# A fused S4D and MLP-mixer kernel: layer 1's operands moved to one place modulo 256 bytes, and a new order of layer 2's products

## The chip, the core and the metric

The kernel runs on one core of one Trainium2 chip. The metric is the device time of one execution in microseconds (us). All names of engines are those of the profile: PE is the matrix engine, PEld its weight loads, DVE the vector engine, ACT the scalar engine with its function tables, POOL the GpSimd engine, SP the sync engine, which here only issues DMAs.

## The reference

For 2048 tokens of 576 features, the reference normalizes the input twice and sends it through two branches. One is an S4D convolution (a long convolution with a kernel made from complex exponentials, done with FFTs), the other a two-layer MLP with a hidden width of 4608. The branches are multiplied and added to the input.

```python
x = A_u                                     # 1 x 2048 x 576, float32
xn = _layernorm(x)
s = S4D(xn, log_A_real, A_imag, C_real, C_imag, log_dt, D_skip)   # FFT convolution over the tokens
y = _layernorm(xn)
h = gelu(einsum("bsd,df->bsf", y, w1) + b1)       # 576 -> 4608, tanh form
g = silu(einsum("bsf,fd->bsd", h, w2) + b2)       # 4608 -> 576
return x + s * g
```

## The kernel before

**The MLP's arithmetic.** A float32 value is cut into a high part, which the matrix engine reads as `float32r`, and a low part, the rest. Every product of two float32 matrices is then three products on PE: high by high, high by low, low by high. `XH` and `XL` are the transposed normalized tokens (four blocks of 128 features), `XR` holds the last 64 features, its high part on partitions 0 to 63 and its low part on 64 to 127. `w1h`, `w1l`, `w1r` and `w1s` are the parts of `w1`, `w2h` and `w2l` those of `w2`, `hh` and `hl` those of the hidden values.

**Slots.** The hidden width is worked off in 12 groups of 384 (`G` = 3 blocks of 128), twice: once for the first 1024 tokens, once for the other 1024. Each group handles two token blocks of 512 (`TB`), so there are 48 slots. A slot has two layers:
- Layer 1 (`layer1`, L512; in slot 0 `first_layer1`, L527 to L533): three hidden blocks, each of 14 matmuls of 128x512. The moving operand is a slice of `XH`, `XL` or `XR`, the stationary one a 128-column slice of `w1h`, `w1l`, `w1r` or `w1s`. These 14 add up in one bank of PSUM. Then `hidden` makes a gelu on ACT (L545), a copy into `hh` on ACT (L548), and a subtraction into `hl` on DVE (L551).
- Layer 2 (`layer2`, L569): for each of four sets `j` of 128 tokens, 18 matmuls of 128x288: three hidden blocks `i` by two halves `dh` of the 576 output columns by the three products of parts. The moving operand is a half row of `w2h` or `w2l`, the stationary one a 128-column slice of `hh` or `hl`. DVE adds the sum to `acc` (L577).

`l2_terms` gives the order of layer 2. For the first two token sets it has four pieces: set 0 with the hidden blocks 0 and 1 (12 matmuls), the beginning of set 1 with them, set 0 with block 2, the rest of set 1. Sets 2 and 3 follow, a half at a time. The reason is that block 2 leaves layer 1 last, so its gelu, copy and subtraction run while the first pieces are multiplied.

**What is fitted in between.** The S4D branch (tables of sines and exponentials on ACT and DVE, small matmuls at L889, L962, L1000, L1053 and L1080, FFT products on DVE) and the splitting of the weights (L489 on DVE, L492 on ACT) are cut into steps, and the class `Order` places them while the kernel is traced. It keeps planned times of each engine. A hidden value's steps are urgent; another step of ACT or DVE is placed only if it would end, by the plan, before the next urgent step of that engine is due (`advance`; the due times come from `hidden_by` and `add_by`, which add up the planned lengths `LEN` of the PE pieces). The resulting order on each engine is fixed; the chip then runs each engine in that order, with waits. The test for ACT charges 1.28 us per table load:

```python
                    if st["tbl"]:
                        d += 1.28 * (1 + (st["tbl"] != self.tbl))
                    if b > horizon or b + d > soon.get(e, 1e9) + st["late"]:
                        continue
```

So a step that names a table pays for one load back, and for one load more if another table is in; a step that names none (copies, absolute values, weight splits) pays nothing.

**Where the operands lie.** The tiles lie in SBUF in the order in which the trace first asks for them. As the kernel is built, `XH`, `XL`, `XR` and `w1s` start 192 bytes past a multiple of 256 in each partition; `w1h`, `w1l` and `w1r` start 64 bytes past one. All slices of them that the matmuls read are whole multiples of 256 bytes further on. `w2h`, `w2l`, `hh` and `hl` start 64 bytes past a multiple of 256; the first half of an output row of `w2h` or `w2l` (`dh` = 0) stays there, and the second half (`dh` = 1) begins 1152 bytes on, at 192.

Of the kernel before, what the change touches and what calls it, by code (L numbers as in the profile page):

```python
# [9 lines left out]
F32 = mybir.dt.float32  # L10
# [7 lines left out]
L, D, N, F = 2048, 576, 128, 4608  # L18
P = 128
# [16 lines left out]
G = 3  # L36
# [18 lines left out]
class Order:  # L55
# [83 lines left out]
    def advance(self, horizon):  # L139
        while True:  # L140
            best = None
            soon = dict(self.next)
            for u in self.urgent:
                st = u[1][0]
                k = (max(u[0], self.t[st["eng"]]), 0)
                if u[0] <= horizon and (best is None or k < best[0]):
                    best = (k, u, None)
                for st in u[1]:
                    soon[st["eng"]] = min(soon.get(st["eng"], 1e9), st["by"])
            for x in self.lines:  # L150
                if x["steps"] and x["steps"][0]["by"] < 1e9:
                    st = x["steps"][0]
                    soon[st["eng"]] = min(soon.get(st["eng"], 1e9), max(st["by"], self.t[st["eng"]] + st["dur"]))
            for n, x in enumerate(self.lines):
                h = self.head(x)
                if h is None or h[0]["eng"] == "PE":
                    continue
                st, r = h
                if st["eng"] is None:
                    k = (max(r, 0), 1 + n)  # L160
                    if r > horizon:
                        continue
                else:
                    e = st["eng"]
                    b = max(self.t[e], r)
                    d = st["dur"]
                    if st["tbl"]:
                        d += 1.28 * (1 + (st["tbl"] != self.tbl))
                    if b > horizon or b + d > soon.get(e, 1e9) + st["late"]:
                        continue  # L170
                    k = (b, 1 + n)
                if best is None or k < best[0]:
                    best = (k, None, x)
            if best is None:
                break
            if best[1] is not None:
                self.go(best[1])
            else:
                self.run(best[2])
            self.pin()  # L180
# [31 lines left out]
def mixer_kernel(ctx, tc, u, log_a_real, a_imag, c_real, c_imag, log_dt, d_skip, w1, b1, w2, b2,  # L212
                 f1, f2, g2, g1, tvals, ident, out, parts=("mlp", "s4d")):
    nc = tc.nc
    sb = ctx.enter_context(tc.tile_pool(name="sb", bufs=1))
# [5 lines left out]
    def bank2(name):  # L221
        return ps.tile([P, 2, TB], F32, name=name, bufs=2 if name == "cv" else 1)
# [6 lines left out]
    def tok(t, b, p0=0, n=P):  # L229
        return dram(t, (b + 16 * p0) * D, [[16 * D, n], [1, D]])  # L230
# [24 lines left out]
    tv, small = tvs[:, :NV], tvs[:, NV:]  # L255
    b1t = sb.tile([P, F // P], F32, name="b1t")
    halfpi, epst = small[:, 0:2], small[:, 2:4]
    w1s = sb.tile([P, G * P], F32R, name="w1s")

    def load_tv():  # L260
# [53 lines left out]
    nc.vector.memset(epst[:, 0:1], EPS)  # L314
    nc.vector.memset(epst[:, 1:2], EPS * EPS)
    nc.vector.memset(w1s[64:].bitcast(F32), 0.0)


    YT, XT = {}, {}
# [28 lines left out]
    def norms(b0, n):  # L348

        def stats(t, part=None):
            if part == 1:
                pass
            elif t == 0 and b0 in (1, 3):
                MV[b0] = SECOND.pop()
            elif t == 0:
                a, r = (UV[:, D + 8 * b0 + 8 * k:D + 8 * b0 + 8 * k + 8] for k in range(2))
                a, r = a.rearrange("p (t k) -> p t k", k=2), r.rearrange("p (k t) -> p k t", k=2)
                MV[b0] = a[:, :n], r[:, :, :n]  # L360
                if n == 1:
                    SECOND.append((a[:, 1:2], r[:, :, 1:2]))
                    PAIR[b0 + 1] = r[:, :, :2]
            if part != 1:
                MV["st"] = sb.tile([P, 2, 6], F32, name="st")
            st = MV["st"]
            for i in range(2) if part is None else (part,):
                nc.vector.bn_stats(st[:, i], XT[b0 + t][:, i * 288:(i + 1) * 288])
            if part != 0:
                nc.vector.bn_aggr(MV[b0][0][:, t], st)  # L370

        def roots():
            mv, rs = MV[b0]
            nc.scalar.activation(rs[:, 0], mv[:, :, 1], AF.Sqrt, bias=epst[:, 0:1], scale=1.0)
            nc.scalar.activation(rs[:, 1], mv[:, :, 1], AF.Sqrt, bias=epst[:, 1:2], scale=1.0 + EPS)

        def recip():
            nc.vector.reciprocal(MV[b0][1], MV[b0][1])

        def second(t):  # L380
            mv, rs = MV[b0]
            y = sb.tile([P, D], F32, name="row", bufs=NROW)
            nc.vector.tensor_scalar(y, XT[b0 + t], mv[:, t, 0:1], rs[:, 1, t:t + 1], op0=OP.subtract, op1=OP.mult)
            if b0 >= 8:
                nc.sync.dma_start(y_s[b0 + t - 8], y)
            else:
                YT[b0 + t] = y

        def first(t):
            mv, rs = MV[b0]  # L390
            x = XT.pop(b0 + t)
            nc.gpsimd.tensor_scalar(x, x, mv[:, t, 0:1], rs[:, 0, t:t + 1], op0=OP.subtract, op1=OP.mult)
            nc.gpsimd.dma_start(tok(xn_s, b0 + t), x)
        return stats, roots, recip, second, first
# [1 line left out]
    XH = sb.tile([P, KB, 2, TB], F32R, name="XH")  # L396
    XL = sb.tile([P, KB, 2, TB], F32R, name="XL")
    XR = sb.tile([P, 2, TB], F32R, name="XR")
    dsk = sb.tile([P, D // 4], F32, name="dsk")
    nc.vector.memset(dsk, 0.0)  # L400

    def y_load(b):
        y = sb.tile([P, D], F32, name="row", bufs=NROW)
# [59 lines left out]
    def w1_tiles():  # L463
        W[1] = (sb.tile([P, KB, G * P], F32R, name="w1h"), sb.tile([P, KB, G * P], F32R, name="w1l"),
                sb.tile([P, G * P], F32R, name="w1r"), w1s)
# [32 lines left out]
    def mx(i):  # L498
        return "mxa" if (turn[0] + i) % 2 == 0 else "mxb"
# [54 lines left out]
    def layer2(g, tb, j, terms, last, alone=False):  # L554

        h, lo = W[2]
        hh, hl = HID[tb]
        c = slice(j * P, (j + 1) * P)  # L560
        if alone and terms[0][1]:
            Q2[j] = bank2("cv")
        elif j not in Q2:
            Q2[j] = bank2(mx(j + 1))
        q = Q2[j]
        for i, dh in terms:
            d = slice(dh * 288, dh * 288 + 288)
            for k, (a, b) in enumerate(((hh, h), (hh, lo), (hl, h))):
                nc.tensor.matmul(q[:, dh, :288], a[:, i, c], b[:, i, d], start=i == 0 and k == 0,  # L569
                                 stop=i == G - 1 and k == 2)  # L570
        if last:
            Q2.pop(j)

        def add(dh, n):
            o = acc[:, tb * 4 + j].rearrange("p (h d) -> p h d", h=2)[:, dh:dh + n]
            b = bias2.rearrange("p (h d) -> p h d", h=2)[:, dh:dh + n]
            nc.vector.tensor_add(o, q[:, dh:dh + n, :288], b if g == 0 else o)  # L577
        return add
# [554 lines left out]
    def warm_up(n):  # L1133
        for _ in range(n):
            nc.tensor.matmul(qb[:, 0], zero[:, :P], zero, start=True, stop=True)
    warm_up(22)
    na = [norms(b, 1) for b in range(4)]
    na[0][0](0)
    w1_tiles()

    nc.gpsimd.tensor_copy(small[:, 4:5], MV[0][0][:, 0, 0:1])
    nc.gpsimd.dma_start(idp, dram(ident, 0, [[P, 64], [64 * P, 2], [1, P]]))
# [43 lines left out]


    L1 = 14 * 0.2315
    LEN = [L1] * G + [3 * n * 0.132 + 0.02 for n in (4, 2, 2, 4, 3, 3, 3, 3)]

    T0 = 12.5
    for e, t in dict(PE=0.0, ACT=4.6, DVE=3.7, POOL=3.8, SP=0.0).items():
# [46 lines left out]
    def weigh_in(which):  # L1239

        m = KB + 1 if which == 1 else G
        end = od.t["PE"] + sum(LEN[G:] if which == 1 else LEN[:G])
        for i in range(m):
# [126 lines left out]
    def l2_terms(k):  # L1370

        if k < 4:
            a = [(i, dh) for dh in range(2) for i in range(G - 1)]
            b = [(G - 1, dh) for dh in range(2)]
            return ((0, a, False, range(G - 1)), (1, a[:2], False, range(G - 1)),
                    (0, b, True, (G - 1,)), (1, a[2:] + b, True, range(G)))[k]
        j, dh = k // 2, k % 2
        return j, [(i, dh) for i in range(G)], dh == 1, range(G)

    def when(pos, q):  # L1380

        return od.t["PE"] + sum(LEN[k % NPOS] for k in range(pos + 1, q))

# [24 lines left out]
    for slot in range(NSLOT):  # L1408
        turn[0] = slot + 1
        g, tb = slot // 2 % NG, slot % 2  # L1410
        n = slot // 2
        final = slot >= NSLOT - 2
        for pos in range(NPOS):
# [19 lines left out]
            else:  # L1433
                j, terms, last, hid = l2_terms(pos - G)
# [8 lines left out]
                halves = slot == NSLOT - 1 and j == 3  # L1443
                od.unit(lambda: cell.append(layer2(g, tb, j, terms, last, halves)), LEN[pos], need)
                look_ahead(pos)
                if last or halves:
                    add = cell[0]
                    dh, k = (terms[0][1], 1) if halves else (0, 2)
                    done = ("acc", slot, j, dh)
                    chain = [step("DVE", dve(288 * k), lambda: add(dh, k), mark=done, by=add_by(pos, j))]  # L1450
                    if final:
                        b = 8 + 4 * tb + j
                        x = el if slot < NSLOT - 1 else od.line()
                        st = finish(b, dh * 288, (dh + k) * 288, slot == NSLOT - 1, slot == NSLOT - 1 and j > 1)
# [69 lines left out]
```

## Time and profile before

| | |
|---|---|
| median of 3 runs (lowest, highest) | 1108.05 us (1106.91, 1109.93) |
| the profiled execution's own time | 1107.08 us |
| its span, first to last instruction | 1105.3 us |
| granted clock of PE | 0.999 |
| busy: PE, PEld, DVE, ACT, POOL | 99%, 85%, 85%, 59%, 18% |

The profile shows one execution. [...] The distance between the starts of two matmuls that follow each other is what one of them costs. The view of waits tells who sat idle and what ended the idle time; the chain tells what the end was waiting for, step by step.

### The profile page before, as it was taken

What the parts mean: (1) busy time and instruction counts of PE and PEld (TensorE: products, weight loads), DVE (VectorE), ACT (ScalarE), POOL (GpSimd) and SP (SyncE); (2) the same over time, 40 slices, a digit from 0 to 9 for tenths busy, and PEclk for the clock granted to TensorE, in tenths of its full rate; (3) what the DMA queues carried; (4) which work ended last, traced back from release to release, by engine and by line L of the source; (5) the groups of instructions that cost most, each with busy time, mean ns of one, the idle gap of its engine ahead of it and who ended that gap; (6) DMA issues with size and microseconds to landing.
All of it is one profiled execution on the core that took longest, in us unless ns stands there. A gap on an engine that the chain in (4) does not pass through costs nothing.

```text
span 1105.3 us, 27245 instructions
## 1 busy us (share of the span) xinstructions
PE 1088.8 (99%) x11547; PEld 941.5 (85%) x11547; DVE 940.9 (85%) x1510; ACT 657.1 (59%) x977; POOL 197.9 (18%) x282
## 2 busy tenths in 40 slices
PE   9999999999999999999999999999999999999997
PEld 7889989888888888888888888888888888888896
DVE  7799698978999999989699998999999976666466
ACT  6666688666656556657866755665764733233333
POOL 5584532011000200010100001000100021110231
PEclk9999999999999999999999999999999999999999
DMA  8645557333233231633322322233412455342254
GB/s 244 224 147 182 192 205 209 103 107 114 65 87 83 72 93 40 140 94 99 106 85 89 69 77 78 67 98 49 125 22 95 109 139 179 87 127 83 60 186 114
DMA packets 111513, 125.54 MB, mean 114 GB/s; under 512 B 59940, under 2 KB 82032, under 8 KB 110368
## 3 DMA queue, kind: packets, MB, share of 16 engines
q1 hardware_dynamic: 95728, 76.44, 24.7%
q0 software_dynamic: 15104, 46.49, 13.6%
q8 instruction: 90, 1.47, 0.5%
q10 hardware_dynamic: 560, 0.89, 0.3%
q14 instruction: 31, 0.25, 0.1%
HBM read 95.52 MB, written 34.01 MB: 117 GB/s over the span
## 4 chain that ended last, share of the span: by engine, by line
PE 84%; DVE 11%; ACT 2%; issue 2%; DMA 1%; SPq 0%; DVEq 0%; ACTq 0%
PE mxb L569 19%; PE mxa L569 19%; PE mxa L512 19%; PE mxb L512 16%; PE cv L889 3%; PE cv L1000 3%; PE cv L1053 2%; PE cv L962 2%; DVE hl L551 1%; DVE w2l L489 1%; DVE acc L577 1%; PE cv L1080 1%; DVE mg L832 1%; DVE A L949 1%; DVE w L807 1%
## 5 line engine op out<-in xcount | busy, mean ns | idle before, releaser
L569 PE MATMUL mxa<-w2h,hl 128*128 128x288 f32 x573 | 170.0, 297 | 4.0 <-DVE hl L551 4.0
L569 PE MATMUL mxb<-w2h,hh 128*128 128x288 f32 x576 | 171.6, 298 | 0.0
L569 PE MATMUL mxa<-w2h,hh 128*128 128x288 f32 x573 | 171.0, 298 | 0.3 <-DVE acc L577 0.3
L569 PE MATMUL mxb<-w2h,hl 128*128 128x288 f32 x576 | 170.2, 296 | 0.0
L569 PE MATMUL mxb<-w2l,hh 128*128 128x288 f32 x576 | 169.5, 294 | 0.0
L569 PE MATMUL mxa<-w2l,hh 128*128 128x288 f32 x573 | 168.6, 294 | 0.0
L551 DVE TENSOR_TENSOR hl<-h,hh 128x512 fp32r<-128x512 f32 x144 | 98.7, 687 | 73.4 <-ACT hh L548 72.9
L789 POOL DMA_DIRECT2D par<-par_s x36 | 27.4, 761 | 533.0 <-DVE mg L832 520.1
L545 ACT ACTIVATE h<-mxa,b1t 128x512 f32<-128x512 f32 x73 | 50.0, 687 | 117.0 <-PE mxa L512 115.1
L569 PEld LDWEIGHTS mxb<-w2h,hh 128*128 128x128 f32 x576 | 108.1, 188 | 8.6 <-issue 2.9
L569 PEld LDWEIGHTS mxa<-w2h,hh 128*128 128x128 f32 x573 | 107.5, 188 | 7.9 <-issue 2.3
L569 PEld LDWEIGHTS mxa<-w2h,hl 128*128 128x128 f32 x573 | 107.6, 188 | 5.6 <-DVE hl L551 5.6
L569 PEld LDWEIGHTS mxb<-w2l,hh 128*128 128x128 f32 x576 | 108.2, 188 | 0.8
L569 PEld LDWEIGHTS mxa<-w2l,hh 128*128 128x128 f32 x573 | 107.7, 188 | 0.8
L569 PEld LDWEIGHTS mxb<-w2h,hl 128*128 128x128 f32 x576 | 108.1, 188 | 0.0
L545 ACT ACTIVATE h<-mxb,b1t 128x512 f32<-128x512 f32 x71 | 48.9, 688 | 91.3 <-PE mxb L512 90.3
L548 ACT ACTIVATE hh<-h 128x512 fp32r<-128x512 f32 x144 | 90.8, 631 | 4.2
L492 ACT ACTIVATE w2h<-raw 128x576 fp32r<-128x576 f32 x72 | 44.5, 675 | 63.2 <-PE mxa L569 63.1
L577 DVE TENSOR_TENSOR acc<-mxb,acc 128x576 f32<-128x576 f32 x88 | 65.8, 748 | 17.5 <-PE mxb L569 17.3
L512 PE MATMUL mxa<-XH,w1h 128*128 128x512 f32 x284 | 79.3, 400 | 0.5 <-DVE acc L577 0.5
L512 PE MATMUL mxb<-XH,w1h 128*128 128x512 f32 x280 | 78.7, 402 | 0.5 <-ACT h L545 0.5
L577 DVE TENSOR_TENSOR acc<-mxa,acc 128x576 f32<-128x576 f32 x88 | 65.4, 743 | 15.9 <-PE mxa L569 15.5
(235 smaller groups left out, 2483.6 us busy)
## 6 DMA issues: line engine op xcount, KB each, us to landing
raw<-in_B_w_dram SPq DMA_DIRECT2D x72, 288.0 KB, 3.2
raw<-in_B_w_dram SPq DMA_DIRECT2D x96, 192.0 KB, 2.9
par_s<-A POOLq DMA_DIRECT2D x8, 1080.0 KB, 4.8
par<-par_s POOLq DMA_DIRECT2D x36, 240.0 KB, 3.3
f2t<-f2q SPq DMA_DIRECT2D x24, 256.0 KB, 3.4
raw<-in_B_w_dram SPq DMA_DIRECT2D x48, 96.0 KB, 3.3
u_s<-in_A_u_dram POOLq DMA_DIRECT2D x16, 288.0 KB, 4.4
xc<-xn_s SPq DMA_DIRECT2D x48, 96.0 KB, 3.9
```

Of the source, the lines that this page charges most:

```text
L492: nc.scalar.activation(h, r, AF.Copy)
L512: nc.tensor.matmul(q, a, b, start=j == 0, stop=j == len(ops) - 1)
L545: nc.scalar.activation(t, q, AF.Gelu_apprx_tanh, bias=b1t[:, g * G + i:g * G + i + 1], scale=1.0)
L548: LAST[0] = nc.scalar.activation(hh[:, i], t, AF.Copy)
L551: nc.vector.tensor_sub(hl[:, i], t, hh[:, i].bitcast(F32))
L569: nc.tensor.matmul(q[:, dh, :288], a[:, i, c], b[:, i, d], start=i == 0 and k == 0, stop=i == G - 1 and k == 2)
L577: nc.vector.tensor_add(o, q[:, dh:dh + n, :288], b if g == 0 else o)
L789: nc.gpsimd.dma_start(PAR[b].rearrange("p (g i) k -> p g (i k)", g=4), dram(par_s, (b // 6 * CH + b % 6 * 4) * NPAR, [[D * NPAR, P], [24 * ...
L889: nc.tensor.matmul(q[32 * g:32 * g + 32, i // 2, i % 2 * 64:i % 2 * 64 + 64], U[:, ri, 4 * g + i, :], v[:, ri, 4 * g + i, :], start=ri == ...
L962: nc.tensor.matmul(Q1ST[i, x][g // 2][64 * f:64 * f + 64, g % 2].rearrange(order), f1t[r].rearrange("p s k -> p (s k)"), rhs(r, f), start= ...
L1000: nc.tensor.matmul(Q[i][32 * q:32 * q + 32, f, 2 * ri:2 * ri + 2], m[r, 4 * i + q, 32 * ri:32 * ri + 32], A2[r, 4 * p + 2 * i + q // 2, :, ...
L1053: nc.tensor.matmul(QI[q // 2][64 * f:64 * f + 64, q % 2, i], MAT["g2t", p + i // 2][r, i % 2, ri], YS[p + i // 2][0][r, i % 2, ri, f], sta ...
```

## The change

Four edits, and the lengths that go with them:
- `dsk` (576 bytes in a partition) is allocated and cleared before `w1s` instead of after `XR`. Everything in between moves up by 576 bytes, which is 64 past a multiple of 256: `w1s`, `XH`, `XL`, `XR`, and with them `A2`, `acc` and `U`, which are used by the S4D branch and the sums.
- The tiles of `w1` are made before the first statistics (`st`, 48 bytes), so that `w1h`, `w1l` and `w1r` move down by 64 bytes. As the changed kernel is built, all seven operands of layer 1 start at a multiple of 256 bytes. `w2h`, `w2l`, `hh` and `hl` stay where they were.
- In layer 2, set 1 takes three (block, half) pairs, nine matmuls, before set 0's last block instead of two pairs, six matmuls. And in each piece the products with the low part of block 2 (`hl`, `i` = 2) come last. `LEN` follows: 4, 3, 2, 3 in place of 4, 2, 2, 4.
- `Order.advance` charges an ACT step for a load if its table is not the one that is in, and for another if the table after it is not that of gelu or silu; a step without a table is charged too, where the table that is in is another than these.

```diff
-                    if st["tbl"]:
-                        d += 1.28 * (1 + (st["tbl"] != self.tbl))
+                    if e == "ACT":
+                        after = st["tbl"] or self.tbl
+                        d += 1.28 * ((after != self.tbl) + (after not in ("gelu", "silu")))
...
+    dsk = sb.tile([P, D // 4], F32, name="dsk")
     w1s = sb.tile([P, G * P], F32R, name="w1s")
...
+    nc.vector.memset(dsk, 0.0)
...
     XR = sb.tile([P, 2, TB], F32R, name="XR")
-    dsk = sb.tile([P, D // 4], F32, name="dsk")
-    nc.vector.memset(dsk, 0.0)
...
-        for i, dh in terms:
+        todo = [(i, dh, k) for i, dh in terms for k in range(3)]
+        todo.sort(key=lambda x: x[0] == G - 1 and x[2] == 2)
+        for i, dh, k in todo:
             d = slice(dh * 288, dh * 288 + 288)
-            for k, (a, b) in enumerate(((hh, h), (hh, lo), (hl, h))):
-                nc.tensor.matmul(q[:, dh, :288], a[:, i, c], b[:, i, d], start=i == 0 and k == 0,
-                                 stop=i == G - 1 and k == 2)
+            a, b = ((hh, h), (hh, lo), (hl, h))[k]
+            nc.tensor.matmul(q[:, dh, :288], a[:, i, c], b[:, i, d], start=i == 0 and k == 0,
+                             stop=i == G - 1 and k == 2)
...
     na = [norms(b, 1) for b in range(4)]
+    w1_tiles()
     na[0][0](0)
-    w1_tiles()
...
-    LEN = [L1] * G + [3 * n * 0.132 + 0.02 for n in (4, 2, 2, 4, 3, 3, 3, 3)]
+    LEN = [L1] * G + [3 * n * 0.132 + 0.02 for n in (4, 3, 2, 3, 3, 3, 3, 3)]
...
-            return ((0, a, False, range(G - 1)), (1, a[:2], False, range(G - 1)),
-                    (0, b, True, (G - 1,)), (1, a[2:] + b, True, range(G)))[k]
+            return ((0, a, False, range(G - 1)), (1, a[:3], False, range(G - 1)),
+                    (0, b, True, (G - 1,)), (1, a[3:] + b, True, range(G)))[k]
```

As the two are built, both have 8571 matmuls and 884 activations; ACT's table loads go from 93 to 98. Since `Order` places its steps anew, the order of the S4D steps and weight splits changes on every engine.

## The prediction

> **What bounds the kernel now.** I read the page first, then the waits of PE, then the chain that ended last, then the timeline around single matmuls, since the page already says that little else is left.
>
> ```profile
> span 1105.3 us, 27245 instructions
> PE 1088.8 (99%) x11547; PEld 941.5 (85%) x11547; DVE 940.9 (85%) x1510; ACT 657.1 (59%) x977; POOL 197.9 (18%) x282
> PEclk9999999999999999999999999999999999999999
> PE 84%; DVE 11%; ACT 2%; issue 2%; DMA 1%; SPq 0%; DVEq 0%; ACTq 0%
> ```
>
> PE is busy 99% of the span at full granted clock, and it carries 84% of the chain. So a gain has two sources only: PE's few waits, or a matmul that takes less time. The waits of PE:
>
> ```profile
> PE mxa L569 <- DVE hl L551: 4.0, 7, 1.2
> PE mxa L1135 <- POOL XL L1129: 1.3, 1, 1.3
> PE cv L1053 <- issue: 1.2, 1, 1.2
> PE mxa L512 <- DVE acc L577: 0.5, 1, 0.5
> ...
> PEld mxa L569 <- DVE hl L551: 5.6, 7, 1.4
> ```
>
> The largest is 4.0 us in seven waits of layer 2 for `hl` (5.6 us seen from the weight loads). All the rest is single events. Then the chain, for what a matmul costs:
>
> ```profile
> 1082.04 3.26 PE mxb L512 x14
> 1085.30 3.25 PE mxa L512 x14
> ```
>
> A hidden block of layer 1 is 14 matmuls in 3.25 us, 232 ns each. There are 48 x 3 = 144 such blocks, 2016 matmuls, 468 us of the span.
>
> **The address edit: what a start address can do.** The trace holds one stretch with 128x512 matmuls of the same type whose moving and stationary operand start at the same place modulo 256 bytes: the warm-up at L1135, which reads one slice of `XL` for both. Once the clock is up:
>
> ```profile
> 6.51 2.43 PE L1135 MATMUL mxa<-XL 128*128 128x512 f32 x10
> ...
> L1135 PE MATMUL mxa<-XL x22: 388/563/793, 1.3 to 8.6; 128*128 128x512 f32 x22
> ```
>
> Ten of them take 2.43 us, of which the last one's own record is 0.39. So nine distances make 2.04 us, 226.7 ns each, against 232. Layer 1 reads its moving operands at 192 and its weights at 64, except that the matmul with `w1r` runs while `w1s` is loaded, and that one lies at 192 like `XR`. These are the only aligned pairs of layer 1; first and last of 141:
>
> ```profile
> 37.84 0.40 PE L512 MATMUL mxa<-XR,w1r 128*128 128x512 f32 x1
> 38.08 0.40 PE L512 MATMUL mxa<-XR,w1s 128*128 128x512 f32 x1
> ...
> 1087.92 0.40 PE L512 MATMUL mxa<-XR,w1r 128*128 128x512 f32 x1
> 1088.15 0.40 PE L512 MATMUL mxa<-XR,w1s 128*128 128x512 f32 x1
> ```
>
> Over the 141 pairs the distance has two levels: 41 times 226 or 227 ns, and about 233 for the other 100, in the mean 231.1. Among the 1853 undisturbed distances of layer 1 (mean 232.1) only 13 others are that short. So the level of the warm-up exists in the kernel and it comes with the alignment, but not always. Layer 2 says the same: at `dh` = 0 both operands lie at 64, at `dh` = 1 the moving one at 192. Starts of six matmuls each, for set 0 with `dh` = 0, set 0 with `dh` = 1, set 1 with `dh` = 0:
>
> ```profile
> 414.59 0.30 PE L569 MATMUL mxa<-w2h,hh 128*128 128x288 f32 x1
> ...
> 415.38 0.29 PE L569 MATMUL mxa<-w2h,hh 128*128 128x288 f32 x1
> ...
> 416.18 0.29 PE L569 MATMUL mxb<-w2h,hh 128*128 128x288 f32 x1
> ...
> 416.97 0.29 PE L569 MATMUL mxa<-w2h,hh 128*128 128x288 f32 x1
> ```
>
> Aligned six take 0.79 us, the others 0.80; over the whole trace 131.7 against 133.1 ns, and single aligned ones fall to 126 or 127, the others hardly ever. What decides is the matmul before. Of the 141 aligned pairs of layer 1, 42 of the 48 whose predecessor took 230 ns were short (counted up to 228 ns), and next to none after another length. In layer 2 an aligned matmul that follows a short one was never short. In the warm-up every one after a short one was short. I read this as a phase between the streaming of the moving operand and the load of the next weights: a short matmul of 512 columns leaves the phase as it was, one of 288 columns shifts it. If so, layer 1, aligned throughout, falls into the short level after a few matmuls of each unbroken run and stays there.
>
> - Ceiling: all of layer 1 at the warm-up's rate. 14 x 0.2267 = 3.174 us per block against 3.25; 144 x 0.076 = 10.9 us gained.
> - Other end: the aligned pairs of layer 1 as they are, 232.1 - 231.1 = 1.0 ns x 2016 = 2 us gained; by layer 2's difference of 1.4 ns, 2.8 us. Below nothing: if the aligned ones stick to the slow level of 233, 0.9 x 2016 = 1.8 us lost.
> - Value: as built, layer 1 of the changed kernel is cut by S4D pieces and layer 2 into 77 unbroken runs. With a short level in 3 of 10 cases at a random phase, a run pays some three long matmuls first: 77 x 3 x 5.4 ns = 1.2 us. That leaves 9.7. I take 8.5, near the warm-up's row, because that is the only row of aligned after aligned at 512 columns, and leave 1.2 for phases that never get there (the warm-up reads zeros from one address, layer 1 does not).
>
> [...]
>
> **Layer 2's order.** Before, the first product with `hl` of block 2 stands behind 12 + 6 + 2 = 20 matmuls of layer 2, now behind 12 + 9 + 4 = 25; at 132 ns (a row of layer 2 stands below) that is 0.66 us later. The planner knows of 9 - 6 = 3 of these (0.40 us through `LEN`) and moves the due times by as much, so the margin that it cannot fill with other work grows by 0.26 us only. The longest of the seven waits:
>
> ```profile
> 1074.04 2.38 PE mxa L569 x18
> ...
> 845.96 0.94 DVE L1021 TENSOR_TENSOR pr<-cv,kk 128x768 f32<-128x768 f32 x1
> 846.94 0.56 DVE L1024 TENSOR_TENSOR pr<-pr,ys 128x384 f32<-128x384 f32 x1
> 847.53 0.36 DVE L1028 TENSOR_TENSOR ys<-pr 128x192 f32<-128x192 f32 x1
> 847.81 0.35 DVE L1029 TENSOR_TENSOR ys<-pr 128x192 f32<-128x192 f32 x1
> 848.08 0.68 DVE L551 TENSOR_TENSOR hl<-h,hh 128x512 fp32r<-128x512 f32 x1
> ...
> 848.81 0.40 PE L569 MATMUL mxa<-w2h,hl 128*128 128x288 f32 x1 [1.17 <-DVE hl L551]
> ```
>
> DVE ran four S4D products first and came to `hl` too late; it is DVE's queue that is late, not ACT. Seven waits shorter by 0.26 to 0.66 us are worth 1.8 to 4.0 us. I take 2.5. The number of products is the same, and putting the `hl` products last costs nothing: they go to two banks that are open anyway. What is late next is the `hl` of set 1, further behind.
>
> **The planner's rule and the rest.** The five added table loads:
>
> ```profile
> L545 ACT ACT_TABLE_LOAD x40 | 51.3, 1283 | 0.9 <-DVE acc L593 0.2
> ...
> PEld mxb L512 <- ACT w2h L492: 3.0, 5, 0.7
> ...
> 600.00:800.00 200.00, 197.50 (x2632) 167.74 (x2631) 188.80 (x292) 129.12 (x186) 16.76 (x26) 1.00 0.31 79
> ```
>
> 5 x 1.283 = 6.4 us of ACT, which is idle for 1105 - 657 = 448 us: 0 on the path as long as they fall into that idle time, 6.4 lost if each stood before a gelu that PE waits for, and at most the 3.0 us of the second row gained. I take 0. The order on DVE is drawn anew, and in the stretch of 600 to 800 us DVE is busy 188.8 of 200 us; a PE that is 1% faster leaves it 2 us less. I take 1.5 us lost in new waits there (0 to 4). `A2` and `U` move too, operands of S4D's small matmuls:
>
> ```profile
> L889 PE MATMUL cv<-v,U 128*32 128x64 f32 x2304 | 39.6, 221 | 0.0
> L1000 PE MATMUL cv<-A,f2t 64*32 64x192 f32 x1536 | 38.7, 332 | 0.2 <-DVE pr L1021 0.2
> ```
>
> The same 5.4 in 232 would be 2% of 78 us, 1.8 us either way; I take 0. The start (12.9 us to the first layer 1) and the 7.5 us behind the last matmul stay.
>
> **The sum.** The profiled execution took 1107.08 us (span 1105.3 and 1.8 around it). 1107.08 - 8.5 - 2.5 + 1.5 = 1097.6. The median of the runs is 0.97 above that execution, so the forecast is 1098.5 us, and its own range 1095 to 1101.5 (the ceiling for layer 1, or 3 us less).
>
> **Rivals.** A measurement of this kernel can tell about 0.3% from no change: 1104.7 to 1111.4 is "the same".
> - *The phase does not hold.* Layer 1 pays the mixed rate of its 141 pairs or of layer 2. 2 to 2.8 us gained there, 2.5 in the waits, 0.5 lost on DVE: about 1103.5. For it: in layer 2 no short matmul follows a short one. Against it: the warm-up, where each does.
> - *The addresses do nothing; the edit does not do what it says.* The short level would then belong to the warm-up's zeros. 0 - 2.5 + 0.5: 1106. Against it: the 41 short pairs, which hold real data. [...]
> - *DVE comes late in every slot.* The new order may put S4D products ahead of `hl` as in the rows above, since the planner fills most of the added margin. The price is the mean of today's seven waits, 4.0/7 = 0.57 us a slot. From 20 more such slots on (11.4 us) it outweighs the two gains; at 27 more, with layer 1 at 8.5 and no gain in the old waits, it is 1108.05 + 15.4 - 8.5 = 1115. For it: 188.8 of 200 us busy. Against it: with the old margin it was seven slots.
>
> **How the numbers follow.** The phase holds: 0.52, 1098.5. It does not hold: 0.22, 1103.5. The addresses do nothing: 0.15, 1106. DVE late: 0.11, 1115. Of the second case some 0.03 lie within 0.3%, so faster 0.71, same 0.18, slower 0.11. The range runs from 1095, the ceiling, to 1107, which takes in the second and nearly all of the third case; outside are the last case and what lies below 1095 or just above 1107, together 0.2.
>
> **What would show it.** Blocks of layer 1 in the chain at 3.18 to 3.20 us instead of 3.25 (step one right), at 3.23 (the first rival) or 3.25 (the second). Waits of PE for `hl` at 1 to 2 us in all. The matmuls of layer 2 as before, 18 in 2.38. The prediction is wrong if PE's waits for DVE exceed 8 us, or if the blocks of layer 1 get longer.

## The result, and the profile after

The changed kernel takes 1111.81 us (median of 7 runs, 1110.80 to 1113.95), the kernel before 1107.93 (7 runs beside it, 1106.91 to 1109.93). The ratio is 1.0037, 95% interval 1.0025 to 1.0049: slower by 0.4%, where 1098.5 was forecast. In the changed kernel layer 1 is L513, the hidden values are L546, L549 and L552, layer 2 is L572 and the sum is L580. First the page: span, busy times, the chain's shares.

```profile
span 1110.0 us, 27233 instructions
PE 1085.3 (98%) x11547; PEld 941.9 (85%) x11547; DVE 942.4 (85%) x1510; ACT 657.6 (59%) x982; POOL 198.6 (18%) x282
...
PE 77%; DVE 15%; ACT 4%; issue 2%; DMA 1%; DVEq 0%; POOL 0%; ACTq 0%
```

PE is busy for 3.5 us less than before (1088.8), and yet the span is 4.7 us longer. PE's share of the chain fell from 84% to 77%, and DVE's rose from 11% to 15%. The chain that ended last shows the matmuls themselves (start, us, what):

```profile
1045.35 3.17 PE mxb L513 x14
1048.53 3.17 PE mxa L513 x14
...
1078.00 2.39 PE mxa L572 x18
...
1085.95 3.17 PE mxb L513 x14
```

A block of layer 1 takes 3.17 us instead of 3.25, and layer 2 is what it was. So the address edit did in layer 1 what was forecast. The waits of PE (us in total, times, longest) show where the time went:

```profile
PE mxa L572 <- DVE hl L552: 4.4, 6, 1.8
PE mxa L572 <- DVE acc L580: 2.8, 6, 0.8
PE mxb L572 <- DVE acc L580: 1.4, 3, 0.7
...
PE mxb L572 <- ACT h L546: 1.2, 1, 1.2
PE cv L418 <- DVE U L381: 1.1, 1, 1.1
...
PE mxa L513 <- DVE acc L580: 1.0, 2, 0.6
PE mxb L513 <- ACT h L546: 0.9, 1, 0.9
PE mxa L572 <- ACT h L546: 0.8, 1, 0.8
```

The wait for `hl` did not shrink (4.0 us before, 4.4 now), and a wait that hardly existed before, PE for the sum `acc`, has come: 5.2 us in eleven waits for 0.8 in two. The bank of PSUM that a sum reads is the one that a later product writes, so that product has to wait for the sum.

I added up, over the whole trace, the distances between the starts of neighbouring matmuls, and split each in two: up to 1.06 times the median of its line and shape it counts as usual, and what goes beyond is excess. (With 1.03 or 1.10 in place of 1.06 the parts move by up to 2.5 us, and the changes in them by half a us at most.) Layer 1's usual distances (1974 matmuls) fell from 459.4 to 451.0 us, by 8.4. The excess rose from 105.8 to 117.9 us, by 12.0, of which 9.5 lie inside layer 2. From the last matmul's start to the end it takes 8.5 us instead of 7.5. All other usual distances together changed by 0.1. That makes the 4.7 us of the span. The excess is more than the waits, because a wait is counted only from the end of the record before it, 0.29 us after that matmul's start in layer 2, where the next would have started after 0.13.

One wait cost more than itself. These are DVE's and then PE's timeline around 151 us, and two windows there (us, busy times, and the granted clock third from the end):

```profile
150.42 1.23 DVE L810 TENSOR_TENSOR w<-par,tv 128x1024 f32<-128x1024 f32 x1 [2.93 <-DMA par<-par_s]
151.56 0.68 DVE L552 TENSOR_TENSOR hl<-h,hh 128x512 fp32r<-128x512 f32 x1
152.30 0.61 PE L572 MATMUL mxa<-w2h,hl 128*128 128x288 f32 x2 [1.81 <-DVE hl L552]
152.71 0.44 PE L572 MATMUL mxb<-w2h,hh 128*128 128x288 f32 x1
152.95 0.44 PE L572 MATMUL mxb<-w2l,hh 128*128 128x288 f32 x1
...
152.00:154.00 2.00, 1.70 (x8) 1.70 (x9) 1.90 (x4) 1.05 (x1) 0.00 (x0) 0.65 0.02 5
154.00:156.00 2.00, 2.00 (x10) 2.00 (x10) 1.71 (x5) 1.14 (x3) 0.00 (x0) 0.50 0.05 12
```

An S4D step was planned ahead of `hl`; it waited 2.93 us for its DMA, `hl` stood behind it in DVE's queue, and PE sat idle for 1.81 us. Then the granted clock fell to half and the matmuls came every 0.24 us instead of 0.13. By the two windows that is 2 x 0.35 + 2 x 0.50 = 1.7 us more.

### The profile page after: what moved, and what is told of

Read it like the earlier page. It is cut to its first block, busy times and chain, and to the rows that moved or that the text cites. A ratio compares the mean times of both kernels' runs of the same rounds, so it can differ in the third digit from the quotient of the medians.

```text
span 1110.0 us, 27233 instructions
## 1 busy us (share of the span) xinstructions
PE 1085.3 (98%) x11547; PEld 941.9 (85%) x11547; DVE 942.4 (85%) x1510; ACT 657.6 (59%) x982; POOL 198.6 (18%) x282
## 4 chain that ended last, share of the span: by engine, by line
PE 77%; DVE 15%; ACT 4%; issue 2%; DMA 1%; DVEq 0%; POOL 0%; ACTq 0%
PE mxb L572 18%; PE mxa L572 18%; PE mxa L513 16%; PE mxb L513 14%; PE cv L892 3%; PE cv L1003 2%; DVE acc L580 2%; PE cv L965 2%; PE cv L1056 1%; DVE hl L552 1%; DVE w2l L490 1%; DVE pr L1024 1%; DVE mg L835 1%; ACT w2h L493 1%; DVE w L810 1%
## 5 line engine op out<-in xcount | busy, mean ns | idle before, releaser
L572 PE MATMUL mxb<-w2h,hh 128*128 128x288 f32 x576 | 171.9, 301 | 2.6 <-DVE acc L580 1.4
L572 PE MATMUL mxa<-w2h,hh 128*128 128x288 f32 x573 | 170.8, 300 | 3.5 <-DVE acc L580 2.8
L572 PE MATMUL mxb<-w2l,hh 128*128 128x288 f32 x576 | 169.0, 296 | 0.0
L572 PE MATMUL mxa<-w2l,hh 128*128 128x288 f32 x573 | 167.9, 295 | 0.0
L572 PE MATMUL mxa<-w2h,hl 128*128 128x288 f32 x573 | 162.0, 296 | 4.4 <-DVE hl L552 4.4
L572 PE MATMUL mxb<-w2h,hl 128*128 128x288 f32 x576 | 162.5, 296 | 0.0
L552 DVE TENSOR_TENSOR hl<-h,hh 128x512 fp32r<-128x512 f32 x144 | 98.7, 687 | 45.4 <-ACT hh L549 44.8
L572 PEld LDWEIGHTS mxb<-w2h,hh 128*128 128x128 f32 x576 | 108.5, 188 | 13.6 <-DVE acc L580 3.2
L572 PEld LDWEIGHTS mxa<-w2h,hh 128*128 128x128 f32 x573 | 107.9, 188 | 12.8 <-DVE acc L580 4.7
L546 ACT ACTIVATE h<-mxa,b1t 128x512 f32<-128x512 f32 x73 | 50.0, 686 | 116.0 <-PE mxa L513 114.3
L572 PEld LDWEIGHTS mxa<-w2h,hl 128*128 128x128 f32 x573 | 105.2, 188 | 5.8 <-DVE hl L552 5.8
L572 PEld LDWEIGHTS mxb<-w2l,hh 128*128 128x128 f32 x576 | 108.6, 189 | 0.6
L572 PEld LDWEIGHTS mxa<-w2l,hh 128*128 128x128 f32 x573 | 107.9, 188 | 0.6
L572 PEld LDWEIGHTS mxb<-w2h,hl 128*128 128x128 f32 x576 | 105.9, 188 | 0.0
L546 ACT ACTIVATE h<-mxb,b1t 128x512 f32<-128x512 f32 x71 | 48.8, 687 | 74.5 <-PE mxb L513 71.9
L549 ACT ACTIVATE hh<-h 128x512 fp32r<-128x512 f32 x144 | 90.6, 630 | 3.3
L580 DVE TENSOR_TENSOR acc<-mxa,acc 128x576 f32<-128x576 f32 x88 | 65.8, 747 | 19.6 <-PE mxa L572 19.3
L580 DVE TENSOR_TENSOR acc<-mxb,acc 128x576 f32<-128x576 f32 x88 | 66.0, 750 | 16.8 <-PE mxb L572 16.2
L513 PE MATMUL mxa<-XH,w1h 128*128 128x512 f32 x284 | 79.1, 400 | 1.0 <-DVE acc L580 1.0
L513 PE MATMUL mxb<-XH,w1h 128*128 128x512 f32 x280 | 78.1, 401 | 0.9 <-ACT h L546 0.9
```

The lines of the kernel that those rows point to most:

```text
L513: nc.tensor.matmul(q, a, b, start=j == 0, stop=j == len(ops) - 1)
L546: nc.scalar.activation(t, q, AF.Gelu_apprx_tanh, bias=b1t[:, g * G + i:g * G + i + 1], scale=1.0)
L549: LAST[0] = nc.scalar.activation(hh[:, i], t, AF.Copy)
L552: nc.vector.tensor_sub(hl[:, i], t, hh[:, i].bitcast(F32))
```

## The experiments

The address edit gains what layer 1 shows, so something else loses more. Three theories of it:
- The new order of layer 2 makes the loss, since DVE now has the time of 9 matmuls instead of 12 for set 0's sum, before set 2's first product needs the bank.
- Not the order but the planner's new lengths make it, since they draw the placement on DVE and ACT anew.
- The planner's rule for tables makes it.

All medians below are beside runs of the kernel before on the same chip, which took 1107.7 to 1108.5 us.

**The parts one at a time.** The address edit alone (the moved `dsk` and `w1_tiles`; the order of every engine's instructions stays that of before):

> The kernel before with the address edit alone: layer 1's operands at a multiple of 256 bytes, order of every engine as before. Theory (the gain of the short matmuls is real and independent, the losses come from the new order): 1107.9 - 8.4 = about 1099.5 us, blocks of layer 1 at 3.17 to 3.20 us, PE's waits as before (4 us for hl). Rival (a faster PE leaves DVE less time, so the address edit itself makes the new waits): 1104 us or more, with several us of PE waits for acc or hl that the kernel before doesn't have.

Measured 1102.72 us, ratio 0.995 (0.9935 to 0.9965): 5.1 us gained. Layer 1's usual distances fell by 8.3 us, as in the whole change. Where a part of the rest went is seen in the waits, a step of the timeline and two windows:

```profile
PE mxa L569 <- DVE hl L551: 5.0, 7, 1.2
PE cv L1053 <- issue: 2.5, 2, 1.9
...
647.57 0.40 PE L1053 MATMUL cv<-ys,g2t 32*64 32x96 f32 x10 [1.91 <-issue]
...
648.00:650.00 2.00, 2.00 (x7) 1.60 (x8) 1.35 (x3) 1.97 (x4) 0.00 (x0) 0.79 0.04 8
650.00:652.00 2.00, 2.00 (x6) 1.62 (x5) 1.26 (x2) 0.84 (x1) 0.00 (x0) 0.50 0.00 0
```

The seven waits for `hl` are longer by 1.0 us in all: PE comes earlier, DVE does not. The idle times of PE at L1053 went from 1.2 us to 2.5; the longest became 1.9, and after it the clock fell to half, which with the window from 652 to 656 us (granted clock 0.93) is 1.7 us again. These are 1.0 + 1.3 + 1.7 = 4.0 us. The execution profiled here is the slowest of the four (1103.89 us), and its span is only 3.2 us shorter than before, so 5.1 of the 8.3 us are missing in it. Whether the clock fell in the other three is not shown.

The change without the address edit; layer 2's edit alone (order and `LEN`); the planner's rule alone:

> The changed kernel without the address edit (the new order of layer 2 and the planner's rule, operands where they were). Theory: 1111.8 + 8.4 = about 1120 us, with the same 4 us of PE waits for acc as the changed kernel. Rival (losses only together with the faster layer 1): 1108 to 1113 us.

> The new order of layer 2 alone (nine products of set 1 first, low part of block 2 last, the planned lengths with it). If the shorter gap between set 0's last product and set 2's first (9 matmuls instead of 12, 1.2 instead of 1.6 us for DVE's sum) makes the losses: 1115 to 1120 us, 3 us or more of PE waits for acc. If the planner's rule makes them: 1105 to 1108 us.

> The planner's rule for ACT's table loads alone. If it makes the losses, by moving S4D steps and weight splits: 1114 to 1120 us and new PE waits for DVE or ACT outside layer 2's acc. If layer 2's order makes them: 1106 to 1110 us.

Measured 1116.46 (ratio 1.0074, 1.0058 to 1.0091), 1116.31 (1.0075, 1.0059 to 1.0090) and 1108.23 (1.0004, 0.9994 to 1.0013). The first and the changed kernel have the same order on DVE and differ by 4.7 us, so the address edit gains about as much within the change as alone, and less than the 8.4 expected. The rule alone leaves the order of instructions on every engine as it is, so it costs nothing, and with layer 2's edit it adds nothing either (1116.46 for 1116.31); that theory falls. Layer 2's edit alone costs 8.5 us, and 8.5 - 5.1 = 3.4 is about the 3.9 of the whole change. The waits of PE with layer 2's edit alone, and a place where one arises, in DVE's queue and then on PE:

```profile
PE mxa L571 <- DVE acc L579: 3.9, 8, 1.1
PE mxa L571 <- DVE hl L551: 3.3, 4, 1.5
...
PE mxb L571 <- DVE acc L579: 1.2, 2, 0.7
...
PE mxa L512 <- DVE acc L579: 0.6, 1, 0.6
...
856.73 0.55 DVE L1019 TENSOR_TENSOR ys<-cv,kk 128x384 f32<-128x384 f32 x1
857.19 0.95 DVE L1023 TENSOR_TENSOR pr<-cv,kk 128x768 f32<-128x768 f32 x1
858.17 0.56 DVE L1026 TENSOR_TENSOR pr<-pr,ys 128x384 f32<-128x384 f32 x1
858.65 0.75 DVE L579 TENSOR_TENSOR acc<-mxa,acc 128x576 f32<-128x576 f32 x1
...
859.46 0.40 PE L571 MATMUL mxa<-w2h,hh 128*128 128x288 f32 x1 [1.06 <-DVE acc L579]
```

S4D products stand ahead of the sum, and PE waits 1.06 us for the bank that the sum reads.

**Order against lengths.** The new order with the old `LEN`, and the old order with the new `LEN`:

```diff
-    LEN = [L1] * G + [3 * n * 0.132 + 0.02 for n in (4, 2, 2, 4, 3, 3, 3, 3)]
+    LEN = [L1] * G + [3 * n * 0.132 + 0.02 for n in (4, 3, 2, 3, 3, 3, 3, 3)]
```

> Layer 2's new order of products (nine of set 1 first, low part of block 2 last) with the old planned lengths, operands where they were, old rule for ACT: DVE, ACT, POOL and SP have the same instructions in the same order as in the kernel before, only PE's matmuls are reordered. If the planner's new placement made the 8.5 us: 1104 to 1108 us, since the low part is needed 0.66 us later and the sums for set 2 have 9 instead of 12 matmuls of time. If the shorter time for the sums made them: 1113 to 1117 us, with 4 us or more of PE waits for acc.

> The counterpart: the old order of products with the new planned lengths (4, 3, 2, 3), so that DVE, ACT, POOL and SP have the order of the kernel with layer 2's edit, and PE the products as before. If the planner's new placement makes the 8.5 us: 1113 us or more, with long PE waits for hl, since the due times lie 0.4 us later than PE asks for it. If the shorter time for the sums makes them: 1108 to 1111 us.

The order without the new lengths: 1108.1 us (ratio 1.000, 0.999 to 1.001). The new lengths without the order: 1119.72 (1.0099, 1.0083 to 1.0115). In the first, DVE, ACT, POOL and SP run the very order of before, and the waits change places:

```profile
PE mxa L571 <- DVE hl L551: 1.7, 4, 0.6
...
PE mxa L571 <- DVE acc L579: 1.1, 3, 0.5
```

The wait for `hl` falls from 4.0 to 1.7 us, as forecast for the order itself; 0.8 come back in the sum (1.6 us with one more wait in layer 1, for 0.8), and 1.3 in a wait for a DMA at the start. So the order by itself changes the time by no more than about 1 us, and the lengths make the loss.

**Both with the address edit.** The address edit with the low part last but the old pieces and lengths, and with the whole new order and the old lengths:

> The address edit and, of layer 2's edit, only the low part of block 2 last within its piece; six products of set 1 first as before, planned lengths as before. The need for hl moves by 2 matmuls, 0.26 us, and the time for the sums stays at 12 matmuls. Both theories: a little below the address edit alone, 1100 to 1102.5 us, waits for hl down from 5 to 3 us, none new for acc.

> The address edit with layer 2's new order and the old planned lengths; DVE, ACT, POOL and SP as in the kernel before. If the planner's new placement was the loss: 1096 to 1101 us, the best so far. If the shorter time for the sums was the loss: 1106 to 1111 us.

Measured 1101.58 (ratio 0.9939, 0.9924 to 0.9954) and 1102.43 (0.9950, 0.9934 to 0.9967). Both beat the kernel before and the changed one. The second lies above the 1096 to 1101 us expected for it and level with the address edit alone (1102.72), so the new order brings no gain that can be told from none, even under the old plan.

**Is it these lengths, or any?** The planned time of one matmul of layer 2 changed by 1 ns, with the old order and lengths and with the new:

```diff
-... 3 * n * 0.132 + 0.02 ...
+... 3 * n * 0.131 + 0.02 ...        (and 0.133)
```

> The kernel before with one number of the planner changed: a matmul of layer 2 is planned at 0.131 instead of 0.132 us. The computation and PE's order inside layer 2 stay; the placement of S4D steps and weight splits is drawn anew. Theory A (the new lengths 4, 3, 2, 3 make a worse plan in themselves: later due times for hl, shorter time for the sums): 1105 to 1111 us. Theory B (any new placement costs or gains several us, and the kernel before has a lucky one): 1112 us or more.

> As the former, with 0.133. Theory A: 1105 to 1111 us. Theory B: 1112 us or more.

> Layer 2's edit alone (order and planned lengths as in the changed kernel, operands and rule as before) with 0.131 instead of 0.132. Theory A: 1114 to 1119 us like the edit alone at 0.132 (1116). Theory B: somewhere between 1106 and 1120, as likely below as above 1113.

> As the former, with 0.133. Theory A: 1114 to 1119 us. Theory B: somewhere between 1106 and 1120 us.

| planned ns per matmul | 131 | 132 | 133 |
|---|---|---|---|
| old order and lengths, us | 1113.72 | 1107.72 | 1112.95 |
| new order and lengths, us | 1117.73 | 1116.31 | 1128.91 |

(1116.31 is the run of layer 2's edit alone from above.) The kernel before sits on a favourable plan: 1 ns to either side costs it 5 to 6 us, with no other change. So another plan can lose that much by being another plan, and the new lengths were slower still in each column. At 133 they were slower than either theory allowed.

**Which part of the plan.** In the new plan block 2's gelu, copy and subtraction are due 3 x 0.132 = 0.396 us later. One run puts that back in layer 2's edit alone, another gives every planned step there 0.40 us more in hand:

```diff
-        n = when(pos, o + (G if i < G - 1 else G + 2))
+        n = when(pos, o + (G if i < G - 1 else G + 2)) - (0.396 if i == G - 1 else 0.0)
```

```diff
-    GAP = 0.17
+    GAP = 0.57
```

> The layer 2 edit alone, with one thing put back in the plan: the last hidden block's copy and subtraction are planned as due 0.396 us earlier, as far behind layer 1 as the old lengths had them. The edit alone ran 1116.31 us (before 1107.8), and the same order with the old lengths 1108.1. If the later due time is the cause (the planner fills the 0.40 us with S4D steps, and hl and the sum behind it come late), PE's waits for hl and acc fall back below 4 us and the time is 1107 to 1111. If any redrawing of the plan costs some 5 us, whatever moves it (as 1 ns more or less per planned matmul did: 1113 to 1114), 1112 to 1115. If the other consequences of the new lengths are the cause (the piece that ends set 0 planned earlier or later for the sums), 1115 to 1119 with the waits unchanged.

> The layer 2 edit alone with the planner's spacing between the end of one engine's step and the start of the next engine's raised from 0.17 to 0.57 us, so every step that others wait for is planned with 0.40 us more in hand. If the new lengths lose because their plan is too tight for the chip, PE's waits for DVE in layer 2 fall below 3 us and the time is 1106 to 1111. If redrawing alone costs, 1112 to 1116. If the time is lost by what is left over at the end (the S4D steps that no longer fit are pushed to the last slots), the waits fall but the end is later: over 1118.

The first: 1107.71 us (ratio 0.9995, 0.9986 to 1.0005); the whole loss is gone. The second: 1111.09 (1.0025, 1.0012 to 1.0038). The waits of the first, then the waits of the second and a window of it:

```profile
PE mxa L571 <- DVE acc L579: 3.8, 5, 1.2
...
PE mxb L512 <- DVE acc L579: 1.1, 1, 1.1
...
PE mxa L571 <- DVE hl L551: 0.2, 1, 0.2
```

```profile
PE mxa L571 <- issue: 1.6, 1, 1.6
...
PE mxa L571 <- DVE hl L551: 1.0, 2, 0.6
PE mxa L571 <- DVE acc L579: 0.9, 2, 0.6
...
632.00:634.00 2.00, 2.00 (x10) 2.00 (x10) 1.51 (x3) 0.00 (x0) 0.00 (x0) 0.50 0.12 43
```

With the due time put back, `hl` is late once, by 0.2 us, while the sum is nearly as late as with the edit alone (4.9 us in all for 5.7). The excess over the usual distances is 105.9 us; with the edit alone it was 114.7, and these 8.8 us are about the difference of 8.6. With the wide spacing both are late by little (1.0 and 1.2 us in all), and time is lost elsewhere: it takes 9.7 us from the last matmul's start to the end instead of 7.5, and after one idle time of 1.6 us in layer 2, in which PE waits for nothing that the profile shows, the granted clock is 0.74, 0.50 and 0.91 in the windows of 2 us from 630 to 636, a loss of 1.7 us.

**The whole change with the due time put back, and the due time moved in the best version.**

> The whole change, with the due time of the last hidden block's copy and subtraction put back by 0.396 us in the plan, as in the run that took the loss of the layer 2 edit away (1107.7 for 1116.3). If the later due time is the whole of the loss, what is left is the address edit: 1107.7 to 1108.5 less 5.1 to 5.3, so 1101 to 1104, and PE's waits for hl under 1 us in all. If the loss in the whole change comes from elsewhere (the planner's rule, or a faster PE in front of the same DVE), 1108 to 1112 with the waits for hl and acc together above 5 us.

> The address edit and the low part last, with the lengths and pieces of before (1101.6 us, waits of PE for hl 3.8 us in 6), and hl planned 0.396 us earlier than there. By the due time theory, slack between the planned and the true need rises from 0.53 to 0.92 us, the same as in the run where the waits for hl fell to 0.2, while set 0's sum keeps its twelve matmuls of time: waits for hl under 1 us, for acc under 1 us, 1097 to 1100. If redrawing the plan costs as it did with 1 ns more or less per planned matmul: 1103 to 1107.

The first: 1101.59 us (ratio 0.9935, 0.9918 to 0.9951), with waits for `hl` of 0.9 us in all. One line of the plan makes the change a gain of 6.9 us instead of a loss of 3.9. The plan is drawn with the planner's rule here and is not that of the run before, so the line took the loss away in two plans. The second, the same line with the old pieces and lengths: 1124.68 (1.0147, 1.0132 to 1.0162), where 1097 to 1107 was expected. Its waits, then steps of the chain that ended last, from the last slot on:

```profile
PE mxa L571 <- DVE hl L551: 2.4, 4, 0.8
PE mxa L571 <- DVE acc L579: 1.8, 3, 1.0
...
1089.98 7.77 DMA A<-s_s
...
1104.68 0.56 POOL out_dram L620
1105.23 1.72 issue
...
1111.01 4.44 DMA row<-g_s
```

At slot 36 it is 14.5 us ahead of the kernel before, at the start of the last slot 1.7 (the address edit with the low part last: 6.0), and its span ends 16.8 us behind: its last matmul starts at 1097.1 us, and from there it takes 24.9 us to the end instead of 7.5. I read this so, and no run shows it apart: what the stricter due time keeps out of the early slots is done late and behind the last, with a DMA of 7.8 us, steps on DVE, stores, and a DMA of 4.4 us. An earlier due time is not better as such.

**Is it the equal place of the two operands that shortens layer 1?** Here only `dsk` is moved, so that `XH`, `XL`, `XR` and `w1s` start at 0 modulo 256 and `w1h`, `w1l`, `w1r` stay at 64; the order of every engine is that of before:

> Half of the address edit: only the 576 bytes in front of w1s are moved, so that the moving operands of layer 1 and w1s start at 0 modulo 256 bytes, w1h, w1l and w1r stay at 64. The order of every engine's instructions is that of the kernel before and of the kernel with the whole address edit. If the equal place of the two operands is what shortens a matmul: the blocks of layer 1 stay at 3.24 to 3.26 us in the chain, layer 1's undisturbed distance at 232 ns, and the time is 1106 to 1109. If a moving operand that starts at a multiple of 256 is enough: blocks of 3.18 and 1101 to 1104, as with the whole edit (1102.7). If it is the new place of A2, acc or U that helped: 1102 to 1105 with blocks of 3.25.

Measured 1109.54 us (ratio 1.0015, 1.0006 to 1.0025). Blocks in its chain:

```profile
1080.96 3.27 PE mxa L512 x14
1084.23 3.26 PE mxb L512 x14
```

Operands 64 bytes apart take 3.27 us, 128 apart 3.25 (before), at one place 3.17. The kernel before's warm-up, which reads one slice of `XL` at 192 for both operands, had the 226.7 ns of a matmul in such a block too, so it is the equal place that counts and not the multiple of 256. Moving one side gains nothing, and of the places of `A2`, `acc` and `U`, which moved here too, no gain shows. This kernel and the address edit alone differ by the place of `w1`'s tiles (and of the small `st`), and by 6.8 us. Last, equal places in layer 2, on top of the address edit with the low part last:

```diff
-            d = slice(dh * 288, dh * 288 + 288)
+            d = slice(CUT[dh], CUT[dh + 1])            # CUT = (0, 320, 576)
...
```

The two parts of a row also get other columns of their PSUM banks, and the sum reads them there.

> The address edit and the order with the low part of block 2 last (1101.6 us), and in layer 2 an output row cut into 320 and 256 columns instead of 288 and 288, so that both parts of a row of w2h and w2l start at 64 modulo 256 like hh and hl. The products and their number stay. If equal places shorten every matmul whose length keeps the phase, and multiples of 64 columns do, layer 2 falls from 18 matmuls in 2.38 us to 2.30 to 2.34 (192 sets: 8 to 15 us) and the time is 1087 to 1095. If only 512 columns keep the phase, layer 2 stays at 2.37 to 2.40 and the time is 1099 to 1104. If a matmul of 256 columns is too short to cover the load of the next weights, layer 2 gets longer: 2.45 and more, 1112 and up.

Measured 1103.83 us (ratio 0.9962, 0.9947 to 0.9976), some 2 us above the same kernel with equal halves:

```profile
1049.91 2.40 PE mxb L573 x18
...
1054.71 3.21 PE mxb L513 x14
1057.91 3.17 PE mxa L513 x14
```

Eighteen products take 2.40 us instead of 2.38, so layer 2 gains nothing from equal places with 320 and 256 columns. That matmuls of 512 columns at one place keep the short distance is shown for layer 1 (14 in 3.17 us); which other lengths would, stays open.

## Why the prediction was wrong

- **Layer 1's term: right.** -8.5 was forecast, -8.4 measured, and blocks of 3.17 us fall below the 3.18 to 3.20 named. The phase holds: of the 1374 undisturbed distances (up to 240 ns) of aligned 512-column matmuls that follow one of 226 or 227 ns, 1370 were again at most 228 ns. The other four, 230 or 231 ns, each lie between two blocks of layer 1. So most of the 2.5 us that are missing to the ceiling of 10.9 lie before the first short matmul of a run, and not in phases that are lost again: a run pays 4.2 longer ones in the mean, 2.2 us in all, where three and 1.2 us had been put down. That it is a phase between the streaming of the moving operand and the load of the next weights was my reading; the runs show the distances and not what sets them. The rival in which the addresses do nothing put 0 for this term; no run shows that 0: blocks took 3.17, 3.25 and 3.27 us at three distances between the operands.
- **Taking that term one for one to the end: wrong by 3.2 us.** Alone it brought 5.1. The sum put no price on a faster PE outside 600 to 800 us: in the one execution that was profiled the seven waits for `hl` grew by 1.0 us, the idle times at L1053 by 1.3, and the clock that fell after one of them cost 1.7.
- **Layer 2's term, -2.5, and DVE's, +1.5 (0 to 4): the steps that failed.** Together they were to give -1.0 and gave +8.5 when run alone. The order by itself did about what was said (`hl` from 4.0 to 1.7 us), and I missed its price: set 0's sum has 9 matmuls of cover instead of 12, 0.8 us. What I named next, the `hl` of set 1, was not next; the sum was. The failing sentence is that the planner "moves the due times by as much, so the margin that it cannot fill ... grows by 0.26 us only". It treats the plan of before as kept, with seven waits a little shorter. New lengths draw the plan anew, and the seven waits are those of a favourable plan. The prediction did say that the order on DVE is drawn anew, but it priced this by a faster PE in one stretch (600 to 800 us) and not by the new plan itself. That price was to be read from no row of before: 1 ns per matmul moves the time by 5 to 6 us, and the plans with the new lengths and the due times that follow from them lie 8 to 21 us above where the addresses are those of before.
- **The rule: right at 0.** Alone it moves no instruction. The added loads come with the new lengths: 101 with them and the old rule, 98 with the new rule, 93 before.
- **The rivals.** Mine on the other side, DVE late, came in part: not in 27 more slots, but in eleven waits for the sum (two before) and six for `hl` (seven before). I gave it 0.11. My own mark for a wrong prediction, over 8 us of PE's waits for DVE, was passed: 11.0 for 5.4 before, from the rows of `hl`, `acc`, `U` and the S4D products.
- **What stays open.** That the later due time makes the loss is shown by one line in two plans. That it does so because it is later, and not only because putting it back draws another plan, is not shown: the same line lost 23 us in another plan, and plans that differ by 1 ns per matmul differ by up to 12.6.

## What to carry to other kernels

Where a planner places work by planned lengths, an edit to a length is a new schedule of every engine, and its price is the spread between neighbouring plans, which a run or two with a length changed by 1 ns shows before anything is concluded from the edit. Run the parts apart, and the new order under the old plan: here 8.4 us in layer 1 (5.1 of them at the end) and a harmless order were hidden under a plan that cost 8.5. And look for operand pairs that could start at one place modulo 256 bytes; for 512 columns it was worth 1.8% of layer 1 here (8.4 of 459.4 us).

## What the runs showed of the hardware

- The distance between 128x512 matmuls depended here on where the two operands start against each other modulo 256 bytes: 3.17 us for 14 at one place, 3.25 at 128 apart, 3.27 at 64 apart. With 320 and 256 columns at one place no such gain was seen: 18 products took 2.40 us instead of 2.38.
- An idle time of PE of 1.81 us (the changed kernel) or 1.91 us (the address edit) was followed by half the granted clock, for a loss of 1.7 us; 1.2 us (before) and 1.7 us (the address edit with the low part last) at the step where the address edit had its 1.91 were not. One of 1.6 us was with the wide spacing, and one of 1.6 us was not with layer 2's edit alone, so the length alone does not decide. One of 2.5 us (the whole change with the due time put back, at 10.7 us) went with a granted clock of 0.83 from 10 to 20 us, a loss of 1.7 us as well. In the changed kernel the stretch at half clock ran from 152.61 to 156.02 us, 3.41 us; the windows of 2 us from 152 on have 0.65, 0.50 and 0.99.
